# Constant matmuls on TensorE ahead of the early jobs' products, in a gated scan followed by a two-level mixture of experts

## The chip, the cores and the metric

One core of a Trainium2 chip. The time is device microseconds of one execution. The engines are called TensorE (PE in the rows, PEld its weight loads), VectorE (DVE), ScalarE (ACT), GpSimd (POOL) and SyncE (SP).

## The reference

Over a batch of 4 sequences of 3648 steps with 256 channels, a gated recurrence gives `y`; its 14592 rows are the tokens of a mixture of experts. Each token takes the best of 4 groups and in it the best of 4 experts, so one of 16 experts, and its row is run through that expert's two products.

```python
for t in range(S):                       # gated scan, f = lb + (1 - lb) * sigmoid(f_logit)
    h = f[:, t] * h + (1 - f[:, t]) * x[:, t]
    y[:, t] = h
# x = y as 14592 tokens
g_idx = argmax(x @ w_group); e_idx = argmax(xg @ w_expert[g])
h  = np.maximum(xg[mask_e] @ w1[g, e], 0.0)       # 256 -> 1024
ye = h @ w2[g, e]                                 # 1024 -> 256
out[tok_idx] = (g_w * e_w)[:, None] * ye
```

## The kernel before

**Two kinds of work run side by side.** The scan and the routing go over 29 units of 512 tokens: load of `zt` (z and x), tanh and affine on ScalarE, gate (L210, L230) and scan `h` (L221) on VectorE, transposes of `h` (L248) and routing products (L262, L273) on TensorE, the routing itself in small VectorE operations (L283 to L339) with a counting product on TensorE (L308 and L309, whose result VectorE reads into `both`, L331), and an indirect store that sorts the tokens' rows by expert into the list `xs`. The experts' work is cut into jobs. There are 16 early jobs (kind "A"), one for each expert, that take the first two to six tiles of 128 tokens of an expert as soon as enough units are routed (the table `EARLY`), and 16 later ones (kind "B") for the rest. Early jobs thus run while the scan goes on, up to about 270 us.

**A job.** Its rows come back from `xs` as `xr` (L760, on SyncE's queue), are transposed on TensorE (L816) and split into a float16 and a bfloat16 part, `xh` and `xl` (L821 ScalarE, L822 VectorE). Its weights come in four pieces `st`, split the same way into `wh` (L775 ScalarE) and `wl` (L776 VectorE). The first product (`m1_step`, L850 to L852, three matmuls for each exact one) fills a PSUM bank `ps_m` with 12 matmuls of 256 columns; ScalarE makes `hh` from it (L855) and VectorE `hl` (L856), and only then is the bank free. There are three such banks in turn (tag "m1"), and a job of 256 tokens needs four, so its fourth bank needs the `hl` of its first. The second product (`m2_step`, L869, 24 matmuls for 128 tokens) reads `hh` and `hl` into a bank of tag "m2" (two in turn). Transposes and routing products take a bank of tag "p" (three in turn).

**Order.** The second product of a job stands in the program behind the first product of the next job. Between the steps `bg_step` puts pieces of the scan and of the next job's preparation in. Up to the preparation of the first job the order on TensorE, VectorE and ScalarE is the program's; after that a scheduler orders these engines, by its own estimates, ahead of the run, and each engine then works its list strictly in order. `tri` and `upto` are two constant 128 by 128 masks in bfloat16, made once at the start.

Of the kernel before, what the change touches and what calls it, by code (L numbers as in the profile page):

```python
# [18 lines left out]
P = 128  # L19
NE = 16  # L20
UNIT = 512
# [19 lines left out]
def gated_scan_moe(ctx: ExitStack, tc, zx, lower, wroute, wexp, out, S):  # L41
    nc = tc.nc
# [5 lines left out]
    KF = F // P  # L48
# [21 lines left out]
    def bank(tag):  # L70
        return ps.tile([P, UNIT], F32, name=f"ps_{tag}", tag=tag, bufs=PS_BUFS[tag])
# [49 lines left out]
    tri = const.tile([P, P], BF16, name="tri")  # L121
    nc.gpsimd.tensor_scalar(out=tri, in0=dmat, scalar1=0.0, scalar2=None, op0=ALU.is_gt)
    upto = const.tile([P, P], BF16, name="upto")
# [548 lines left out]
    def make_job(kind, idx):  # L672
        j = Job()
        j.kind, j.idx = kind, idx
        j.len = EARLY[idx][1] * P if kind == "A" else CAPS[idx] if kind == "B" else P
        j.tiles = -(-j.len // P)
        j.chunks, j.pieces, j.cols, j.parts = [], [], [], []
        at = 0
        while at < j.len:
            rest = j.len - at  # L680
            w = 2 * P if rest > 3 * P else P if rest > 2 * P else rest
            n = UNIT // w
            j.cols.append([list(range(c, min(KF, c + n))) for c in range(0, KF, n)])
            j.pieces += [(b, min(2 * P, at + w - b)) for b in range(at, at + w, 2 * P)]
            parts, b = [], at
            while b < at + w:
                m = at + w - b
                g = 1 if m > 96 else 2 if m > 32 else 4
                parts.append((b, min(m, P // g), g))
                b += P // g  # L690
            j.chunks.append((at, w))
            j.parts.append(parts)
            at += w
        j.wh, j.wl, j.st = {}, {}, {}
        j.hh, j.hl = {}, {}
        j.xh, j.xl = {}, {}
        return j
# [134 lines left out]
    def w2_at(ws, c):  # L832
        return ws[2 + c // 4][:, (c % 4) * D:(c % 4 + 1) * D]

    def m1_step(j, ch, cs):
# [11 lines left out]
        for n, c in enumerate(cs):  # L847
            po = pm[:, n * w:(n + 1) * w]
            for k in range(KD):
# [6 lines left out]
        nc.vector.scalar_tensor_tensor(out=j.hl[ch][:, cs[0]:cs[-1] + 1, 0:w], in0=pv, scalar=0.0, in1=hi,  # L856
                                       op0=ALU.max, op1=ALU.subtract)

    def m2_step(j, ch, t):
        b, p, g = j.parts[ch][t]  # L860
        pm = bank("m2")
        c0 = b - j.chunks[ch][0]
        q, dw = P // g, D // g
        n = p if g == 1 else q
        ts = slice(c0, c0 + n)
        for c in range(KF):
            for s, (h, w) in enumerate(((j.hh, j.wh), (j.hh, j.wl), (j.hl, j.wh))):
                for i in range(g):
                    nc.tensor.matmul(pm[i * q:i * q + n, 0:dw], h[ch][:, c, ts], w2_at(w, c)[:, i * dw:(i + 1) * dw],  # L869
                                     start=(c == 0 and s == 0), stop=(c == KF - 1 and s == 2),  # L870
                                     tile_position=(0, i * q) if g > 1 else None)
        o = mo.tile([P, D], F32, name="o", bufs=O_BUFS)
        if j.kind == "B":
            lt, r = j.info, b // P
            if g > 1:
                r += j.tails.index((b, p, g))
        else:
            pi = max(i for i, (a, _) in enumerate(j.pieces) if a <= b)
            lt, r = j.meta[pi], (b - j.pieces[pi][0]) // P
        s = slice(0, p if g == 1 else P)  # L880
        nc.scalar.activation(o[s, 0:dw], pm[s, 0:dw], AF.Copy, scale=lt.bitcast(F32)[s, r, 1:2])  # L881
        nc.gpsimd.indirect_dma_start(  # L882
            out=out_v[out_n[0]].rearrange("n (g d) -> (n g) d", g=g),
            out_offset=bass.IndirectOffsetOnAxis(ap=lt[s, r, 0:1], axis=0),
            in_=o[s, 0:dw], in_offset=None, bounds_check=g * N - 1, oob_is_err=False)
        out_n[0] += 1
# [22 lines left out]
    def bg_pop():  # L909
        done[0] += 1  # L910
        bgq.popleft()()

    def bg_to(n):
        while done[0] < n:
            bg_pop()

    def fetch_to(n):
        while pptr[0] < min(n, len(pieces)):
            j, i = pieces[pptr[0]]
            if j.kind != "A":  # L920
                bg_to(marks["order"])
            job_weights(j, i)
            pptr[0] += 1
# [3 lines left out]
    def prep_thunks(j):  # L927
        th = []

        def sp(i):  # L930
            if i == 2:
                live[0] += 1
            fetch_to(piece_index[(id(j), i)] + STG_BUFS)
            job_split(j, i)
            if i == 3 and j.kind == "B" and j.idx == 1:
                leftovers()
            if i == 3 and j.kind == "B" and j.idx + 1 < NE:
                tail_blank(j.idx + 1)

        for i in range(4):  # L940
            f = lambda i=i: sp(i)
            f.held = i == 2
            th.append(f)
        for pi in range(len(j.pieces)):
            th.append(lambda pi=pi: job_xt(j, pi))
        return th

    def start_macro(mi):
        mac = macros[mi]
        bg_to(marks[EARLY[mac[0].idx][0]] if mac[0].kind == "A" else marks["order"])  # L950
        for j in mac:
            if j.kind != "A" or j.idx == NE - 1:
                job_rows(j)
# [30 lines left out]
    with tc.manual_schedule(engines={mybir.EngineType.PE, mybir.EngineType.DVE, mybir.EngineType.Activation}):  # L984
        for u, n in EARLY_FETCH:
            while u not in last_load:
                bg_pop()
            fetch_to(n)
        bg_to(first)
        start_macro(0)  # L990
        prep = prep_thunks(macros[0][0])
        bg_to(marks["begun"])
        for t in prep:
            t()
    pending = None
    for mi, mac in enumerate(macros):
        q = deque()
        if mi + 1 < len(macros):
            start_macro(mi + 1)
            for j in macros[mi + 1]:  # L1000
                q.extend(prep_thunks(j))
        left = work(mac)
        for j in mac:
            for ch in range(len(j.chunks)):
                for cs in j.cols[ch]:
                    m1_step(j, ch, cs)
                    left -= len(cs)
                    bg_step(q, left - 2, len(cs))
                if pending is not None:
                    pj, pc = pending  # L1010
                    for t in range(len(pj.parts[pc])):
                        m2_step(pj, pc, t)
                        left -= 1
                        bg_step(q, left - 2, 1)
                    if pc == len(pj.chunks) - 1:
                        live[0] -= 1
                pending = (j, ch)
        while q:
            q.popleft()()
    pj, pc = pending  # L1020
    in_order.enter_context(tc.manual_schedule(engines={mybir.EngineType.Pool}))
    for t in range(len(pj.parts[pc])):
        m2_step(pj, pc, t)
    left = nc.values_load(regs["left"][0:1, 0:1], min_val=0, max_val=NT)
    in_order.close()
    with tc.For_i(0, left, 1) as it:
        ent = mo.tile([1, 3], I32, name="ent")
        rem = mo.tile([P, 1], F32, name="rem")
        sync.dma_start(out=ent, in_=tab[bass.ds(it + len(EXTRA_AT), 1), :])
        sync.dma_start(out=rem, in_=tab.bitcast(F32)[bass.ds(it + len(EXTRA_AT), 1), 2:3].broadcast_to([P, 1]))  # L1030
        j = make_job("X", 0)
        regs["tabs"], regs["xrem"] = ent, rem
        job_rows(j)
        for i in range(4):
            job_weights(j, i)
        for i in range(4):
            job_split(j, i)
        job_xt(j, 0)
        for cs in j.cols[0]:
            m1_step(j, 0, cs)  # L1040
        m2_step(j, 0, 0)
# [44 lines left out]
```

## Time and profile before

| | |
|---|---|
| time, median of 3 runs | 774.7 us (774.45 to 777.17) |
| the profiled execution | 776.18 us, span 774.4 us |
| TensorE busy | 715.7 us, 92% of the span |
| VectorE busy | 538.7 us, 70% |
| ScalarE busy | 461.4 us, 60% |
| mean granted TensorE clock | 0.96 |

A group of rows below is one view of the trace of that execution; times in it count from the start of its span. A matmul's busy time is longer than the step from one start to the next, since matmuls overlap; the step is what counts for a sum.

### The profile page before, as it was taken

Reading aid. Unit: us, or ns where it says so; the run is one execution under the profiler, and the core shown is the slowest. Engines: PE = TensorE matmul, PEld = TensorE weight load, DVE = VectorE, ACT = ScalarE, POOL = GpSimd, SP = SyncE. Lnnn points to the kernel's source line nnn. Section 1 sums busy time; section 2 is a strip of 40 time slices with the busy share of each in tenths; the row PEclk is TensorE's granted clock in tenths of the full one; section 3 lists DMA queues with packets and bytes.
Section 4 is the critical chain, followed back from the end, with each engine's and each line's share of the span. In section 5 each row is a group of like instructions: output and inputs, shape, how many; then the busy total and the mean of one; then the engine's idle time right before and its main releaser. Section 6 shows DMA issues by size and latency. Waiting matters only on the chain.

```text
span 774.4 us, 20888 instructions
## 1 busy us (share of the span) xinstructions
PE 715.7 (92%) x8112; PEld 634.0 (82%) x8112; DVE 538.7 (70%) x1058; ACT 461.4 (60%) x824; POOL 289.4 (37%) x272
## 2 busy tenths in 40 slices
PE   2655679999999999999999999999999999999995
PEld 1434567888888888989988898999999999999995
DVE  6889899999999966865555544555564676656540
ACT  6667777987888846454455444454555465555541
POOL 3671264577556453541211222213222322232222
PEclk9955889999999999999999999999999999999998
DMA  7997879999998826378535344453563555555300
GB/s 276 355 347 262 313 245 344 328 314 354 336 311 301 271 96 185 122 238 215 123 116 126 129 99 129 114 129 118 140 173 96 166 151 173 165 164 173 86 30 24
DMA packets 93157, 151.75 MB, mean 196 GB/s; under 512 B 52417, under 2 KB 62559, under 8 KB 89728
## 3 DMA queue, kind: packets, MB, share of 16 engines
q1 hardware_dynamic: 78080, 99.90, 43.5%
q0 software_dynamic: 11424, 30.02, 11.0%
q10 hardware_dynamic: 3552, 20.48, 7.3%
q8 instruction: 64, 1.05, 0.6%
q14 instruction: 37, 0.30, 0.1%
HBM read 112.69 MB, written 38.19 MB: 195 GB/s over the span
## 4 chain that ended last, share of the span: by engine, by line
PE 56%; DVE 19%; DMA 11%; issue 7%; ACT 3%; POOL 2%; SPq 1%; POOLq 0%; DVEq 0%; ACTq 0%
PE ps_m L869 28%; PE ps_m L850 6%; DVE wl L776 6%; PE ps_m L851 6%; PE ps_m L852 6%; DMA zt<-in_zx_dram 5%; DVE h L221 4%; PE ps_p L850 3%; PE ps_p L851 3%; PE ps_p L852 3%; DVE hl L856 3%; DMA st<-in_wexp_dram 2%; DVE zt L210 2%; DMA xs<-blank 2%; POOL out_dram L882 2%
## 5 line engine op out<-in xcount | busy, mean ns | idle before, releaser
L869 PE MATMUL ps_m<-wh,hl 128*128 128x256 f16 (+2 forms) x1320 | 265.7, 251 | 4.7 <-DVE hl L856 4.6
L869 PE MATMUL ps_m<-wl,hh 128*128 128x256 bf16 (+2 forms) x1320 | 265.7, 251 | 0.1
L869 PE MATMUL ps_m<-wh,hh 128*128 128x256 f16 (+2 forms) x1320 | 265.4, 252 | 0.2 <-ACT hh L855 0.2
L869 PEld LDWEIGHTS <-hh 128*128 128x128 f16 (+2 forms) x2640 | 195.6, 99 | 23.6 <-issue 3.3
L850 PE MATMUL ps_m<-xh,wh 128*128 128x256 f16 (+11 forms) x782 | 197.4, 263 | 2.7 <-DVE hl L856 2.7
L851 PE MATMUL ps_m<-xl,wh 128*128 128x256 bf16 (+11 forms) x782 | 197.4, 262 | 1.0 <-DVE xl L822 1.0
L852 PE MATMUL ps_m<-xh,wl 128*128 128x256 f16 (+11 forms) x782 | 197.4, 262 | 0.0
L776 DVE TENSOR_TENSOR wl<-st,wh 128x1024 bf16<-128x1024 f32 x128 | 154.3, 1219 | 51.3 <-ACT wh L775 51.1
L343 POOL DMA_INDIRECT xs<-rows,posi x114 | 133.3, 1169 | 123.8 <-DVE rows L325 45.3
L882 POOL DMA_INDIRECT out_dram<-o,info x75 | 86.1, 1148 | 242.5 <-ACT o L881 214.3
L856 DVE SCALAR_TENSOR_TENSOR hl<-ps_m,hh 128x512 bf16<-128x512 f32 (+6 forms) x176 | 117.4, 670 | 70.3 <-ACT hh L855 69.9
L855 ACT ACTIVATE hh<-ps_m 128x512 f16<-128x512 f32 (+6 forms) x176 | 103.5, 588 | 72.5 <-PE ps_m L852 70.7
L775 ACT CAST wh<-st 128x1024 f16<-128x1024 f32 x128 | 132.1, 1046 | 14.1 <-PE ps_m L869 7.6
L869 PEld LDWEIGHTS <-hl 128*128 128x128 bf16 (+2 forms) x1320 | 104.6, 99 | 15.3 <-DVE hl L856 5.0
L850 PEld LDWEIGHTS <-wh 128*128 128x128 f16 x1088 | 107.2, 99 | 11.0 <-issue 1.6
L851 PEld LDWEIGHTS <-wh 128*128 128x128 f16 x1088 | 107.4, 99 | 10.5 <-issue 2.4
L852 PEld LDWEIGHTS <-wl 128*128 128x128 bf16 x1088 | 107.2, 98 | 9.4 <-issue 1.2
L882 POOL DMA_INDIRECT out_dram<-o,meta x55 | 65.5, 1192 | 111.6 <-ACT o L881 101.0
L881 ACT ACTIVATE o<-ps_m,info 128x256 f32<-128x256 f32 (+4 forms) x75 | 33.1, 441 | 83.8 <-PE ps_m L869 74.3
L850 PE MATMUL ps_p<-xh,wh 128*128 128x256 f16 (+13 forms) x306 | 73.3, 252 | 0.0
L851 PE MATMUL ps_p<-xl,wh 128*128 128x256 bf16 (+13 forms) x306 | 73.3, 252 | 0.0
L852 PE MATMUL ps_p<-xh,wl 128*128 128x256 f16 (+13 forms) x306 | 73.3, 252 | 0.0
(145 smaller groups left out, 741.2 us busy)
## 6 DMA issues: line engine op xcount, KB each, us to landing
st<-in_wexp_dram SPq DMA_DIRECT2D x128, 512.0 KB, 7.2
zt<-in_zx_dram ACTq DMA_DIRECT2D x19, 1024.0 KB, 7.5
zt<-in_zx_dram SPq DMA_DIRECT2D x7, 1024.0 KB, 9.8
xs<-blank SPq DMA_DIRECT2D x26, 258.0 KB, 4.4
xr<-xs SPq DMA_DIRECT2D x19, 258.0 KB, 6.0
xr<-xs SPq DMA_DIRECT2D x17, 129.0 KB, 4.1
xs<-rows,posi POOLq DMA_INDIRECT x114, 7.1
zt<-xs SPq DMA_DIRECT2D x8, 152.0 KB, 3.2
```

The costliest lines, as they stand in the source:

```text
L221: nc.vector.tensor_tensor_scan(out=h[:, k, c0 - a:c1 - a], data0=ff[:, k, c0 - a:c1 - a], data1=uu[:, k, c0 - a:c1 - a], initial=init, op0 ...
L343: sc = nc.gpsimd.indirect_dma_start(out=xs_v[G["t0"] + t][:, :], out_offset=bass.IndirectOffsetOnAxis(ap=R["posi"][:, t:t + 1], axis=0), i ...
L775: nc.scalar.copy(j.wh[i], j.st[i])
L776: nc.vector.tensor_tensor(out=j.wl[i], in0=j.st[i], in1=j.wh[i], op=ALU.subtract)
L850: nc.tensor.matmul(po, w1_at(j.wh, k, c), xh[:, k], start=(k == 0), stop=False)
L851: nc.tensor.matmul(po, w1_at(j.wh, k, c), xl[:, k], start=False, stop=False)
L852: nc.tensor.matmul(po, w1_at(j.wl, k, c), xh[:, k], start=False, stop=(k == KD - 1))
L855: nc.scalar.activation(hi, pv, AF.Relu)
L856: nc.vector.scalar_tensor_tensor(out=j.hl[ch][:, cs[0]:cs[-1] + 1, 0:w], in0=pv, scalar=0.0, in1=hi, op0=ALU.max, op1=ALU.subtract)
L869: nc.tensor.matmul(pm[i * q:i * q + n, 0:dw], h[ch][:, c, ts], w2_at(w, c)[:, i * dw:(i + 1) * dw], start=(c == 0 and s == 0), stop=(c == ...
L881: nc.scalar.activation(o[s, 0:dw], pm[s, 0:dw], AF.Copy, scale=lt.bitcast(F32)[s, r, 1:2])
L882: nc.gpsimd.indirect_dma_start(out=out_v[out_n[0]].rearrange("n (g d) -> (n g) d", g=g), out_offset=bass.IndirectOffsetOnAxis(ap=lt[s, r, ...
```

## The change

A function `keep_warm` puts `n` matmuls of the two constants (128 columns, bfloat16) into the last quarter of a bank, whose result nobody reads. It is called with 46 ahead of the first job's preparation, with 48 in the middle of the second product of the first job (first tile, into a bank "p" of its own), and with 24 at the head of the second product of the second and of the third job (first tile, into the bank that the product then fills). 142 matmuls and as many weight loads are added. The lists of the engines change with them.

```diff
@@ -856,14 +856,23 @@
         nc.vector.scalar_tensor_tensor(out=j.hl[ch][:, cs[0]:cs[-1] + 1, 0:w], in0=pv, scalar=0.0, in1=hi,
                                        op0=ALU.max, op1=ALU.subtract)
 
+    def keep_warm(pm, n):
+
+        for _ in range(n):
+            nc.tensor.matmul(pm[:, UNIT - P:UNIT], tri, upto, start=True, stop=True)
+
     def m2_step(j, ch, t):
         b, p, g = j.parts[ch][t]
         pm = bank("m2")
+        if j.kind == "A" and j.idx in (1, 2) and t == 0:
+            keep_warm(pm, 24)
         c0 = b - j.chunks[ch][0]
         q, dw = P // g, D // g
         n = p if g == 1 else q
         ts = slice(c0, c0 + n)
         for c in range(KF):
+            if j.kind == "A" and j.idx == 0 and t == 0 and c == KF // 2:
+                keep_warm(bank("p"), 48)
             for s, (h, w) in enumerate(((j.hh, j.wh), (j.hh, j.wl), (j.hl, j.wh))):
                 for i in range(g):
                     nc.tensor.matmul(pm[i * q:i * q + n, 0:dw], h[ch][:, c, ts], w2_at(w, c)[:, i * dw:(i + 1) * dw],
@@ -990,6 +999,7 @@
         start_macro(0)
         prep = prep_thunks(macros[0][0])
         bg_to(marks["begun"])
+        keep_warm(bank("m2"), 46)
         for t in prep:
             t()
     pending = None
```

**TensorE, ahead of the first job.** L248 and L262 are transposes and routing of the scan, L816 the transposes of the first job's rows. Before:

```order
L262 MATMUL ps_p<-h,wr 32x128 x8
L273 MATMUL ps_p<-ident,rs 128x128
L248 MATMUL ps_p<-ident,h 128x128 x8
L816 MATMUL ps_p<-ident,xr 128x128 x4
L248 MATMUL ps_p<-ident,h 128x128 x4
L262 MATMUL ps_p<-h,wr 32x128 x8
L850 LDWEIGHTS wh_813
```

Of the change (L862 is `keep_warm`):

```order
L273 MATMUL ps_p<-ident,rs 128x128
L248 MATMUL ps_p<-ident,h 128x128 x8
L862 LDWEIGHTS tri
L862 MATMUL ps_m_813<-upto,tri 128x128
...
L862 MATMUL ps_m_813<-upto,tri 128x128
L816 MATMUL ps_p<-ident,xr 128x128 x4
L248 MATMUL ps_p<-ident,h 128x128 x4
L262 MATMUL ps_p<-h,wr 32x128 x8
```

The 46 stand between the last transposes of the scan and those of the first job's rows.

**TensorE, at the third job's first product.** The program's 48 of the first job's second product come here. The numbers in the names differ between the two kernels: `ps_m_1492` and `ps_m_1550` of before are `ps_m_1588` and `ps_m_1646` of the change, the third job's first and second bank. Before:

```order
L262 MATMUL ps_p<-h,wr 32x128 x8
L850 LDWEIGHTS wh_1291
L850 MATMUL ps_m_1492<-xh,wh_1291 128x256
L850 LDWEIGHTS wh_1291
L850 MATMUL ps_m_1550<-xh,wh_1291 128x256
L248 MATMUL ps_p<-ident,h 128x128 x4
L851 LDWEIGHTS wh_1291
L851 MATMUL ps_m_1492<-xl,wh_1291 128x256
```

Of the change:

```order
L850 LDWEIGHTS wh_1338
L850 MATMUL ps_m_1588<-xh,wh_1338 128x256
L850 LDWEIGHTS wh_1338
L850 MATMUL ps_m_1646<-xh,wh_1338 128x256
L862 LDWEIGHTS tri
L862 MATMUL ps_p<-upto,tri 128x128
...
L862 MATMUL ps_p<-upto,tri 128x128
L248 MATMUL ps_p<-ident,h 128x128 x4
L851 LDWEIGHTS wh_1338
L851 MATMUL ps_m_1588<-xl,wh_1338 128x256
```

The 48 stand between the first matmul into the second bank and the L248 transposes, ahead of the other eleven matmuls of each bank.

**VectorE, from the fourth job's weight splits on.** `wl` is a weight split (L776), the rows from `both` to `rows` are the twelve small operations of the routing, `hl` from `ps_m_1492`, `ps_m_1550` and `ps_m_1595` is that of the third job's first three banks (`ps_m_1588`, `ps_m_1646` and `ps_m_1691` of the change). Before:

```order
L776 TENSOR_TENSOR wl_1510<-st,wh_1509 128x1024
L776 TENSOR_TENSOR wl_1516<-st,wh_1515 128x1024
L856 SCALAR_TENSOR_TENSOR hl<-ps_m_1492,hh 128x512
L776 TENSOR_TENSOR wl_1568<-st,wh_1567 128x1024
L856 SCALAR_TENSOR_TENSOR hl<-ps_m_1550,hh 128x512
L776 TENSOR_TENSOR wl_1574<-st,wh_1573 128x1024
L331 TENSOR_TENSOR both<-ps_p,both 128x32
...
L325 RECIPROCAL rows<-s_1627 128x4 x2
L856 SCALAR_TENSOR_TENSOR hl<-ps_m_1595,hh 128x512
L210 SCALAR_TENSOR_TENSOR zt<-zt 128x1024
L822 TENSOR_TENSOR xl<-ps_p,xh 128x512
```

Of the change:

```order
L776 TENSOR_TENSOR wl_1606<-st,wh_1605 128x1024
L776 TENSOR_TENSOR wl_1612<-st,wh_1611 128x1024
L776 TENSOR_TENSOR wl_1664<-st,wh_1663 128x1024
L776 TENSOR_TENSOR wl_1670<-st,wh_1669 128x1024
L331 TENSOR_TENSOR both<-ps_p,both 128x32
...
L325 RECIPROCAL rows<-s_1723 128x4 x2
L856 SCALAR_TENSOR_TENSOR hl<-ps_m_1588,hh 128x512
L856 SCALAR_TENSOR_TENSOR hl<-ps_m_1646,hh 128x512
L856 SCALAR_TENSOR_TENSOR hl<-ps_m_1691,hh 128x512
L210 SCALAR_TENSOR_TENSOR zt<-zt 128x1024
```

The two `hl` that stood between and behind the last weight splits now stand behind these and behind the routing operations, next to the third.

## Rows read from the trace of the kernel before

**Rows 1.** The page's first part, busy time of each engine with its share of the span, and the granted TensorE clock in 40 slices, in tenths of full speed.
```profile
PE 715.7 (92%) x8112; PEld 634.0 (82%) x8112; DVE 538.7 (70%) x1058; ACT 461.4 (60%) x824; POOL 289.4 (37%) x272
...
PEclk9955889999999999999999999999999999999998
```

**Rows 2.** Busy time by stretch (us from the span's start): the stretch, its length, then for TensorE, its weight load, VectorE, ScalarE and GpSimd the busy us and instructions, then granted clock, share of the DMA engines and GB/s.
```profile
68.00:77.00 9.00, 8.39 (x48) 6.07 (x49) 9.00 (x11) 6.07 (x12) 0.00 (x0) 0.50 0.81 247
...
90.00:101.00 11.00, 6.20 (x36) 4.55 (x33) 10.19 (x19) 5.01 (x12) 8.48 (x8) 0.53 0.73 230
101.00:115.00 14.00, 10.78 (x99) 8.12 (x98) 13.79 (x29) 12.26 (x23) 9.05 (x7) 0.88 0.75 234
115.00:126.00 11.00, 9.00 (x67) 7.32 (x66) 11.00 (x14) 9.14 (x17) 3.26 (x4) 0.84 1.00 344
126.00:274.00 148.00, 146.31 (x1526) 129.87 (x1525) 144.95 (x269) 121.09 (x226) 90.38 (x71) 1.00 0.91 316
274.00:720.00 446.00, 445.54 (x5261) 405.06 (x5260) 263.80 (x528) 230.20 (x393) 127.45 (x114) 1.00 0.51 144
```

**Rows 3.** Who waited for whom: engine, tile and line, what it waited for, then us in total, times, longest. The first five rows are of 65 to 126 us (TensorE's for row loads, for `hl` and for `xl`, and VectorE's for TensorE), the last two are all of TensorE's from 126 to 274.
```profile
PE ps_p L816 <- DMA xr<-xs: 8.8, 3, 5.7
PE ps_m L869 <- DVE hl L856: 4.6, 1, 4.6
...
PE ps_m L850 <- DVE hl L856: 1.1, 1, 1.1
PE ps_m L851 <- DVE xl L822: 1.0, 1, 1.0
...
DVE both L331 <- PE ps_p L309: 2.2, 2, 1.6
...
PE ps_m L850 <- DVE hl L856: 1.2, 2, 0.9
PE ps_p L262 <- DVE both L331: 0.4, 1, 0.4
```

**Rows 4.** TensorE's instructions in order of time: start, us, line, operation, output and inputs, count, and in brackets the idle time ahead with what ended it.
```profile
60.53 1.92 PE L248 MATMUL ps_p<-ident,h 128*128 128x128 f32 x8
68.17 1.32 PE L816 MATMUL ps_p<-ident,xr 128*128 128x128 f32 x4 [5.72 <-DMA xr<-xs]
...
72.91 0.37 PE L851 MATMUL ps_m<-xl,wh 128*128 128x256 bf16 x1
...
74.57 0.42 PE L850 MATMUL ps_m<-xh,wh 128*128 128x256 f16 x1
74.78 0.42 PE L851 MATMUL ps_m<-xl,wh 128*128 128x256 bf16 x1
```

**Rows 5.** VectorE's instructions around the first `both` of the early jobs, columns as above.
```profile
79.17 0.42 DVE L301 TENSOR_TENSOR_SCAN scn<-rmask,oh 128x128 bf16<-128x128 bf16 x1
81.19 0.19 DVE L331 TENSOR_TENSOR both<-ps_p,runoff 128x32 f32<-128x32 f32 x1 [1.59 <-PE ps_p L309]
```

**Rows 6.** TensorE's instructions around the third early job's four banks (the first at 114.55, the second at 115.98, the fourth at 123.70) and the first matmul of the fourth job at 132.29.
```profile
115.98 0.27 PE L850 MATMUL ps_m<-xh,wh 128*128 128x256 f16 x1 [1.15 <-DVE hl L856]
116.09 0.60 PE L248 MATMUL ps_p<-ident,h 128*128 128x128 f32 x4
117.71 0.27 PE L851 MATMUL ps_m<-xl,wh 128*128 128x256 bf16 x1 [1.03 <-DVE xl L822]
...
123.70 0.27 PE L850 MATMUL ps_m<-xh,wh 128*128 128x256 f16 x1
...
132.29 0.27 PE L850 MATMUL ps_m<-xh,wh 128*128 128x256 f16 x1
```

**Rows 7.** VectorE's instructions over the same time; `hl` at 122.86 is that of the third job's first bank (`ps_m_1492`), at 124.59 of its second, at 128.14 of its third.
```profile
120.61 2.34 DVE L776 TENSOR_TENSOR wl<-st,wh 128x1024 bf16<-128x1024 f32 x2
122.86 0.69 DVE L856 SCALAR_TENSOR_TENSOR hl<-ps_m,hh 128x512 bf16<-128x512 f32 x1
123.46 1.22 DVE L776 TENSOR_TENSOR wl<-st,wh 128x1024 bf16<-128x1024 f32 x1
124.59 0.69 DVE L856 SCALAR_TENSOR_TENSOR hl<-ps_m,hh 128x512 bf16<-128x512 f32 x1
125.19 1.22 DVE L776 TENSOR_TENSOR wl<-st,wh 128x1024 bf16<-128x1024 f32 x1
126.33 0.19 DVE L331 TENSOR_TENSOR both<-ps_p,both 128x32 f32<-128x32 f32 x1
...
128.14 0.66 DVE L856 SCALAR_TENSOR_TENSOR hl<-ps_m,hh 128x512 bf16<-128x512 f32 x1
```

**Rows 8.** TensorE's instructions, first and last of 48 matmuls with 128 columns that follow one another without a pause.
```profile
191.73 0.22 PE L850 MATMUL ps_m<-xh,wh 128*128 128x128 f16 x1
...
194.35 0.22 PE L852 MATMUL ps_m<-xh,wl 128*128 128x128 f16 x1
```

**Rows 9.** Busy time by stretches of 5 us, columns as in group 2: two around pauses of TensorE and one ahead.
```profile
45.00:50.00 5.00, 4.30 (x32) 2.93 (x32) 4.79 (x12) 3.31 (x9) 3.86 (x4) 0.50 1.04 402
...
90.00:95.00 5.00, 0.76 (x8) 0.31 (x4) 4.83 (x9) 2.77 (x7) 3.72 (x4) 0.56 0.84 260
95.00:100.00 5.00, 4.44 (x23) 3.50 (x24) 4.36 (x8) 1.24 (x4) 3.78 (x5) 0.50 0.59 176
100.00:105.00 5.00, 4.34 (x45) 3.24 (x43) 4.86 (x15) 4.85 (x10) 1.86 (x2) 0.92 0.48 183
```


## The prediction

> **What bounds the kernel now.** Three views, in this order. The page says how full the engines are: TensorE is busy for 92% of the span and VectorE for 70% [rows 1]. That is an average, so the second view cuts the span where it changes character [rows 2]. Before 126 us TensorE is never full, and the granted clock stands at 0.50 to 0.88 of full speed. VectorE is full: 9.00 of 9.00 us from 68 to 77, 13.79 of 14 and 11.00 of 11 from 101 to 126. From 126 to 274 both are full (146.31 and 144.95 of 148). After 274 TensorE alone is full, 445.54 of 446 us. So whatever TensorE is late by at 274 arrives at the end undiminished, and before 126 a faster TensorE wins only where VectorE waited for it. The third view names those waits [rows 3]. From 65 to 126 TensorE loses 8.8 us to row loads (`xr<-xs`), 4.6 and 1.1 us to VectorE's `hl` and 1.0 us to its `xl`; VectorE loses 2.2 us to TensorE. From 126 to 274 TensorE waits 1.2 us for `hl` and 0.4 us for `both`, and that is all.
>
> The profiled execution took 776.18 us with a span of 774.4, 1.8 us lying around it; its time is 1.5 us above the median of 774.7. I work out a difference on that execution and add it to the median.
>
> **The change part by part.** It adds 142 matmuls, 128 columns wide in bf16, and removes nothing. A matmul of that width at full clock starts 0.0557 us after the one before: 48 of them between 191.73 and 194.35 [rows 8]. At half clock 256 columns take 0.213 us (74.57 to 74.78), so 128 take 0.107 [rows 4].
>
> *The first 46.* TensorE ends its transposes at 62.4 and starts the next at 68.17, after 5.72 us of waiting for a load; 46 at 0.107 us take 4.9 us and end at 67.3 [rows 4]. Cover is complete: cost 0. Were the load 2 us earlier, 1.1 us would show. What can they win? The matmuls behind them wait for VectorE's `xl` until 72.91 anyway [rows 4]. Only then could a higher clock help, and what it helps is `both`: VectorE has its scan done at 79.6, waits 1.59 us for L309 and goes on at 81.19 [rows 5]. If the clock is still full at 72.9, nearly all of that goes: -1.3 us. If not, the order puts three more matmuls of 0.11 us ahead of L308: +0.3 us. I take -0.5, near the middle but closer to nothing. The reason: between 45 and 50 us TensorE was busy for 4.30 of 5 us with transposes and routing work and the clock stayed at 0.50 [rows 9], and it is just such work that stands between the 46 and 72.9. The Trainium skill says likewise, in "TensorE: Matmul & The Clock Gate", Part 4: PE-mode transpose, that transposes don't count as a busy engine does; the trace agrees with its 0.50 at 4.30 busy. By that rule alone the term would be +0.3 and the time 0.8 us longer than mine.
>
> *The 48.* They were written into the first job's second product, where TensorE stood 4.6 us for `hl` [rows 3], but the order puts them later: behind the first matmul into `ps_m_1646`, which is `ps_m_1550` of before, at 115.98 [rows 6]. What waits is behind them on TensorE: the L248 transposes and the remaining matmuls of the third job. There the cover is the 1.03 us wait for `xl`; the 48 take 48 x 0.0557 = 2.7 us at full clock. TensorE also worked at half clock for a while: 0.84 granted over the 11 us from 115 to 126 is 1.8 us short of full [rows 2], and most of that may be spared. So by itself this part costs little. But the order of VectorE changes with it. Before, it made `hl` from `ps_m_1492` at 122.86 between the weight splits, ending 123.5, and TensorE's fourth bank of that job (`ps_m_1651`), which needs that bank back, starts at 123.70: it was just in time [rows 6, 7]. Now two more splits and twelve small routing operations come first. VectorE has no pause here, so times follow by adding: splits done at 122.86, two more of 1.13 (123.46 to 124.59) to 125.12, the small ones 1.81 (126.33 to 128.14) to 126.93, and `hl` 0.67 to 127.6 [rows 7]. TensorE gets there about 123.9 (116.09 + 2.7, then the work of before from 117.71 to 123.70 without its half-clock loss of 1.7, and two L248 groups of 0.44 ahead of it) and stands for 3.7 us. Its fourth bank starts at 127.65: **+3.95 us**. Bounds: 0 if VectorE is 4 us earlier by then, which its 2.2 us of waits don't allow, and +4.3 with the +0.3 from above.
>
> *The 24 of the second job.* Three are ahead of that stall and hidden in it. The other 21 come behind: 1.17 us. The wait of 0.4 for `both` is gone and the L248 group of 0.44 us now lies in the stall: together **+0.3 us**.
>
> *The 24 of the third job* stand ahead of 48 matmuls in a stretch where TensorE has no pause: 24 x 0.0557 = **+1.3 us**, with no cover.
>
> *What comes back.* TensorE being the late one, its 1.2 us of waits for `hl` until 274 go: **-1.2 us**; at worst none of it comes back.
>
> *The clock behind the new stall.* The row of 90 to 95 us, with a pause of 4.6 us in it, shows 0.56, the next 0.50 and the third 0.92 [rows 9]: from the end of the pause at 95.56 to about 100.8 TensorE ran at half rate, which cost 2.6 us. So 0 to 2.6; I take **+0.8**, since the new pause is shorter and the matmuls right behind it are dense.
>
> Sum: -0.5 + 3.95 + 0.3 + 1.3 - 1.2 + 0.8 = +4.65 us; 774.7 + 4.7 = **779.4 us**. With the lower bounds but the stall kept: -1.3 + 3.95 + 0.3 + 1.3 - 1.2 + 0 = +3.0; with the upper (+0.3, +2.6): +7.2.
>
> **The rivals.**
> *The additions only fill.* If VectorE reaches the moved `hl` as TensorE does (it makes up its 2.2 us, or the wait of TensorE for its bank is shorter than I count), the 96 late matmuls cost 5.35 us, less 1.0, 0.4 and 1.2 us of waits that they fill, 1.7 us of half clock and 0.5: +0.5, **775.2 us**. For it: VectorE's total of work is unchanged. Against: its rows from 115 to 128 leave no gap. It decides if the `hl` in question ends before about 125.
>
> *Faster.* TensorE's clock is what matters from 68 to 126. At full clock throughout, 4.2 us come back of 8.39 busy from 68 to 77, 2.5 from 90 to 101, 1.7 of 14 at 0.88 and 1.8 of 11 at 0.84 [rows 2]: 10 us, less the 3.7 us of late matmuls without a wait to fill: -6.3, **768.4 us**. The Trainium skill, in the same page under "Why this matters for your kernels", advises to keep TensorE busy and without long pauses so that it keeps its full rate; by that rule this is the case. Against: VectorE is full in each of those stretches and its order is fixed, so TensorE could not use what it gained beyond VectorE's 2.2 us of waits. It decides if VectorE can be ahead of now by over 4 us at 126.
>
> *Stalls that breed.* TensorE 4.3 us late hands `hh` of the fourth job over late, VectorE, in order, stands about 2.9 us (adding on from 127.6 it would reach that `hl` near 135.9, and TensorE's bank, begun at 132.29 + 4.3, gives `hh` near 138.8), and routing and splits behind it are late; if this comes back to TensorE once more with its half-rate price, 2.8 us are added: **782.2 us**. Against: the banks later on have some us to spare once TensorE is the late one.
>
> **How the numbers follow.** Forecast case 0.45 (776.9 to 781.5), only filling 0.30, breeding stalls 0.16, faster 0.09. A measurement here tells about 0.5% from no change, 3.9 us: 770.8 to 778.6 is "same". Of the forecast case two thirds lie above 778.6. Slower: 0.30 + 0.16 = 0.46; same: 0.15 + 0.29 = 0.44; faster: 0.09 and 0.01 of the filling case, 0.10. The range of 773.0 to 783.0 leaves out the faster case and the far end of the breeding one, some 0.14.
>
> **What would show it.** Right: 46 short matmuls between 62.4 and 67.4 with the load still ending the wait at about 68; the 48 between 115 and 119; TensorE idle 2 to 4 us before an L850, ended by `hl` L856, around 124 to 128; a lower granted clock in the 5 us behind that; TensorE 4 to 6 us behind before at 145 us, and no waits for `hl` until 274. Wrong: no such idle time; or the wait at L331 around 81 gone and VectorE over 2 us ahead at 115; or TensorE waiting for `hl` again at several places after 150.

## The result, and the profile after

The change is slower: 781.87 us, median of 7 runs (780.44 to 785.03), against 776.34 us for the kernel before in 7 runs. The medians differ by 5.5 us; the ratio of the runs is 1.0086, 95% interval 1.0069 to 1.0104, some 6.7 us. The forecast was 4.65 us on a base of 774.7, which 26 later runs put at 775.88. The profiled execution took 782.97 us with a span of 781.2, 6.8 us more than the one before. A ratio leaves out runs over 1.5% above the fastest of their kernel, which takes away a third of the runs of the kernel before where it takes 817 us (10 of 29 and 6 of 20), so that ratios from there can differ from those of the medians by up to 0.8%.

The page's first part of the change, busy time by engine and the granted clock in 40 slices (before: [rows 1]):

```profile
PE 723.7 (93%) x8254; PEld 642.4 (82%) x8254; DVE 539.1 (69%) x1058; ACT 462.6 (59%) x824; POOL 289.1 (37%) x272
...
PEclk9999779999999999999999999999999999999998
```

Busy time by stretch of the change, columns as in [rows 2]; the last two stretches end 6 and 7 us later than there, as the work does:

```profile
68.00:77.00 9.00, 6.15 (x60) 4.90 (x61) 9.00 (x10) 7.26 (x13) 0.00 (x0) 1.00 0.84 250
90.00:101.00 11.00, 7.06 (x41) 5.32 (x42) 10.19 (x20) 5.80 (x13) 8.26 (x8) 0.57 0.69 197
101.00:115.00 14.00, 10.07 (x78) 7.49 (x76) 13.79 (x30) 11.44 (x21) 9.32 (x8) 0.76 0.74 252
115.00:126.00 11.00, 9.57 (x121) 8.48 (x121) 11.00 (x21) 10.56 (x20) 3.55 (x3) 1.00 1.02 388
126.00:280.00 154.00, 151.07 (x1576) 133.86 (x1576) 145.28 (x261) 120.16 (x221) 88.59 (x71) 0.99 0.86 295
280.00:727.00 447.00, 446.55 (x5271) 405.99 (x5270) 263.52 (x528) 231.33 (x396) 127.40 (x114) 1.00 0.51 146
```

The clock of 68 to 77 us went from 0.50 to 1.00, and VectorE, which sets the pace there, was full before and is full now. Behind 280 us nothing differs but the start.

The mean clocks of the two executions (0.960 before, 0.983 now) can't be compared: the clock record of this trace begins at 65.3 us, that of the trace before at 29.1, and a stretch without a record counts as full. The fourth slice above shows a 9, but the eight transposes ahead of the 46 take as long as at the 0.50 of before (1.92 us, [rows 4]):

```profile
61.49 1.91 PE L248 MATMUL ps_p<-ident,h 128*128 128x128 f32 x8
63.19 3.74 PE L862 MATMUL ps_m<-upto,tri 128*128 128x128 bf16 x46
```

TensorE's instructions of the change from the third early job's third bank on, and where the two groups of 24 end up, columns as in [rows 6]:

```profile
122.78 0.64 PE L816 MATMUL ps_p<-ident,xr 128*128 128x128 f32 x4
124.80 0.66 PE L248 MATMUL ps_p<-ident,h 128*128 128x128 f32 x4 [1.38 <-DVE both L331]
125.29 0.33 PE L862 MATMUL ps_m<-upto,tri 128*128 128x128 bf16 x3
...
127.08 0.37 PE L850 MATMUL ps_m<-xh,wh 128*128 128x256 f16 x1 [1.13 <-DVE hl L856]
127.25 0.42 PE L851 MATMUL ps_m<-xl,wh 128*128 128x256 bf16 x1
127.47 0.42 PE L852 MATMUL ps_m<-xh,wl 128*128 128x256 f16 x1
...
130.49 1.35 PE L862 MATMUL ps_m<-upto,tri 128*128 128x128 bf16 x21
...
137.35 0.27 PE L850 MATMUL ps_m<-xh,wh 128*128 128x256 f16 x1
...
144.73 1.50 PE L862 MATMUL ps_m<-upto,tri 128*128 128x128 bf16 x24
...
194.44 0.27 PE L850 MATMUL ps_m<-xh,wh 128*128 128x256 f16 x1 [1.41 <-DVE hl L856]
```

The fourth bank, at 123.70 before [rows 6], starts at 127.08, and TensorE stands twice in front of it: for `both`, then for `hl`. The matmuls behind it follow at 0.21 us, half rate, where they stood at 0.11. The fourth job starts at 137.35 against 132.29.

VectorE's instructions of the change over the same time (before: [rows 7]):

```profile
120.03 4.60 DVE L776 TENSOR_TENSOR wl<-st,wh 128x1024 bf16<-128x1024 f32 x4
124.56 0.18 DVE L331 TENSOR_TENSOR both<-ps_p,both 128x32 f32<-128x32 f32 x1
...
126.37 1.85 DVE L856 SCALAR_TENSOR_TENSOR hl<-ps_m,hh 128x512 bf16<-128x512 f32 x3
...
139.49 0.69 DVE L856 SCALAR_TENSOR_TENSOR hl<-ps_m,hh 128x512 bf16<-128x512 f32 x1 [3.69 <-ACT hh L855]
```

Four splits in a row, then the routing, then three `hl`: VectorE loses nothing by it until 130 us. At 139.49 it has waited 3.69 us for the `hh` of a bank that TensorE began late. The waits of 126 to 280 us, TensorE's and VectorE's:

```profile
PE ps_m L850 <- DVE hl L856: 2.7, 3, 1.4
...
DVE hl L856 <- ACT hh L855: 5.5, 4, 3.7
```

TensorE's 1.2 us for `hl` [rows 3] have become 2.7, of which 1.13 belong to the stall itself. Behind it, the longest wait of before (0.9 us, at 273.7 us) is gone, and one of 1.41 at 194.44 has come.

**Where the time went.** Start against start of the same work, after less before, in the two profiled executions: VectorE 0.95 later at 60 us, ahead of the first added matmul, and 0.70 at 66 us; 0.58 earlier from 82 us on, once its wait in front of `both` is down from 1.59 [rows 5] to 0.32; TensorE 0.45 earlier at the third job's third bank, 3.38 later at the fourth, 5.06 at the fourth job, 6.40 behind the third job's 24, 7.6 over most of 200 to 240 us, 6.86 from 281 us to the end.

### The profile page after: what moved, and what is told of

Same layout as the page of the kernel before. It is cut to its first block, busy times and chain, and to the rows that moved or that the text cites. A ratio compares the mean times of both kernels' runs of the same rounds, so it can differ in the third digit from the quotient of the medians.

```text
span 781.2 us, 21168 instructions
## 1 busy us (share of the span) xinstructions
PE 723.7 (93%) x8254; PEld 642.4 (82%) x8254; DVE 539.1 (69%) x1058; ACT 462.6 (59%) x824; POOL 289.1 (37%) x272
## 4 chain that ended last, share of the span: by engine, by line
PE 62%; DVE 15%; DMA 10%; issue 8%; ACT 2%; POOL 2%; SPq 1%; POOLq 0%; DVEq 0%; ACTq 0%
PE ps_m L878 30%; PE ps_m L850 7%; PE ps_m L852 7%; PE ps_m L851 7%; DMA zt<-in_zx_dram 4%; DVE wl L776 3%; DMA st<-in_wexp_dram 3%; PE ps_p L850 3%; PE ps_p L851 3%; PE ps_p L852 3%; DVE h L221 3%; DVE hl L856 2%; POOL out_dram L891 2%; DVE zt L210 1%; PE ps_p L248 1%
## 5 line engine op out<-in xcount | busy, mean ns | idle before, releaser
L776 DVE TENSOR_TENSOR wl<-st,wh 128x1024 bf16<-128x1024 f32 x128 | 154.3, 1218 | 52.6 <-ACT wh L775 52.4
L891 POOL DMA_INDIRECT out_dram<-o,meta x55 | 63.8, 1160 | 127.3 <-ACT o L890 110.4
```

Of the source, the lines that this page charges most:

```text
L776: nc.vector.tensor_tensor(out=j.wl[i], in0=j.st[i], in1=j.wh[i], op=ALU.subtract)
L891: nc.gpsimd.indirect_dma_start(out=out_v[out_n[0]].rearrange("n (g d) -> (n g) d", g=g), out_offset=bass.IndirectOffsetOnAxis(ap=lt[s, r, ...
```

## The experiments

Two questions: is it the matmuls or the order that they brought with them, and which part of the order. So that the second can be asked without the first, most kernels hold TensorE, VectorE and ScalarE to a written list by edges that fix the order and add no wait:

```
+    def pin(order):
+        for eng, seq in order.items():
+            mine = [i for i in traced if i.engine == eng]
+            for a, b in zip(seq, seq[1:]):
+                tc.add_manual_dep(mine[b], mine[a].name, <order only>)
```

"Old lists" are those of before (but for one or two exchanged neighbours), "new lists" those of the change; the size of each of the four groups is set apart. Held lists keep the second job's 24 together.

Six runs (old_lists_all, new_lists_one, hl_put_back, first46 and the second run of the first and the last) fell on chips on which the kernel before takes 776 us, twelve on chips on which it takes 811 to 817 us. On the slower chips TensorE stands all over the trace without waiting for anything that the profile shows ("issue"): in the change run there, 9.1 us in the second products behind 280 us alone. The trace of the kernel before is that of a 776 us run and has no such wait behind 126 us. So each ratio is taken against the kernel before on the same chip, and each place in a trace is compared after VectorE's shift just ahead of it is taken off.

**Order or matmuls.** old_lists_all: old lists, all 142.

```
+    pin({PE: OLD, DVE: OLD, Activation: OLD})
```

> All 142 matmuls as in the change, at the same places of TensorE's list, but TensorE, VectorE and ScalarE are held, by order-only edges, to the lists that these engines have when each of the four groups is a single matmul; those are the lists of the kernel before but for one or two exchanged neighbours. So this prices the matmuls without the new order. My theory (the new order makes the loss): the sum of the case of only filling, +0.5 us, to +1.5 if the spared half clock of 1.7 us does not come; ratio 1.000 to 1.002; TensorE's fourth bank of the third job less than 1.5 us later than before. Rival (the matmuls themselves are the loss, the order only follows): +5 to +7 us, ratio 1.006 to 1.009.

778.77 us, ratio 1.0040 (1.0025 to 1.0056). TensorE's trace:

```profile
114.66 0.27 PE L916 MATMUL ps_m<-xh,wh 128*128 128x256 f16 x1 [0.98 <-DVE hl L922]
114.77 2.84 PE L947 MATMUL ps_p<-upto,tri 128*128 128x128 bf16 x48
...
122.28 0.27 PE L916 MATMUL ps_m<-xh,wh 128*128 128x256 f16 x1
...
131.95 0.27 PE L916 MATMUL ps_m<-xh,wh 128*128 128x256 f16 x1
```

No stall: the fourth bank at 122.28 is 1.42 us ahead of before, as the second bank was by 1.32 in front of the 48. The second job's 24 take that to 0.33 ahead at the fourth job, the third job's 24 to 1.01 behind at 146 us, and it stays at 1.0 to the end. (This execution, 777.25 us, is 1.5 us under the median.)

new_lists_one: new lists, four matmuls in all.

```
+    pin({PE: NEW, DVE: NEW, Activation: NEW})
-        keep_warm(bank("m2"), 46)
+        keep_warm(bank("m2"), 1)
...
-                keep_warm(bank("p"), 48)
+                keep_warm(bank("p"), 1)
```

and the 24 likewise.

> The counterpart: the three engines are held to the lists of the change, but each group is one matmul (4 in all instead of 142). So this prices the new order without the matmuls. My theory: TensorE still stands 3 to 5 us before the third job's fourth bank, its clock falls behind that stall, and the kernel is 3.5 to 6 us slower than before, ratio 1.0045 to 1.008. Rival (the matmuls are the loss): 0 to 1 us slower, ratio under 1.0015.

782.49 us, ratio 1.0085 (1.0063 to 1.0108): all of the change's loss, with 4 of its 142 matmuls. TensorE's two waits are there, the first longer since no 48 stand in front:

```profile
124.91 0.66 PE L311 MATMUL ps_p<-ident,h 128*128 128x128 f32 x4 [2.79 <-DVE both L394]
...
127.19 0.37 PE L913 MATMUL ps_m<-xh,wh 128*128 128x256 f16 x1 [1.24 <-DVE hl L919]
```

So the order makes the loss, and the matmuls in their places add little to it, though the clock was at half for longer behind this stall than in the change (0.51 against 0.66 from 126 to 131 us), which may make up for some of their cost. In the old lists they cost more than nothing; a repeat, old_lists_all_b:

> The kernel of old_lists_all again. Theory (46 and 48 free, 24 and 24 cost 2.4 us): ratio 1.0015 to 1.0045. Rival (nothing but filling: 0.5 us): 1.001 or less.

778.53 us, ratio 1.0029 (1.0014 to 1.0043), some 2 to 3 us as expected. Its profiled execution, 782.80 us and the slowest of the 12, shows the other end: the clock was 0.50 from 115.8 to 122.6 us, the 48 took 5.33 us instead of 2.84, and the fourth bank started 3.50 us later than before where VectorE was 0.93 later. So the 48 are covered at full clock and not at half.

**Which part of the order.** hl_put_back: the change, with two `hl` back in their old places on VectorE (and, by the holding, all 24 of the second job in front of the bank, which its expectation does not say). VectorE's held list:

```
 wl split 1, wl split 2
+hl of the first bank
 wl split 3
+hl of the second bank
 wl split 4
 both L331, the routing
-hl of the first bank, hl of the second bank
 hl of the third bank
```

> The change with all 142 matmuls and its lists, but with the hl of the third job's first and second bank put back on VectorE to where the kernel before has them, behind the second and behind the third of the four weight splits; nothing else moves. The prediction made this one instruction the stall of 3.95 us. If that is right, TensorE's fourth bank starts near 124 us, and the time is 3 to 4 us under the change, about 778 us, ratio to before 1.002 to 1.004. Rival, from the trace of the change: TensorE first waits for both L331 at 124.80 us, in front of an L248 group that the new list puts ahead of that bank, and with two hl of 0.6 us ahead of it both comes 1.2 us later; then L248 starts near 126.0, the fourth bank near 127.15 against 127.08, and the time stays within 0.7 us of the change, ratio 1.008 to 1.0095.

779.82 us, ratio 1.0052 (1.0034 to 1.0070). At the bank:

```profile
123.20 1.50 PE L944 MATMUL ps_m<-upto,tri 128*128 128x128 bf16 x24
125.77 0.41 PE L325 MATMUL ps_p<-h,wr 128*32 128x128 f32 x2 [1.07 <-DVE both L394]
126.11 0.28 PE L913 MATMUL ps_m<-xh,wh 128*128 128x256 f16 x1
```

`hl` is done at 122.7 and the bank still starts at 126.11: 2.41 us later than before where VectorE is 0.79 ahead, 3.2 in all, against 3.96 in the change. `both`, which now comes behind the two `hl`, holds it. That is the rival's cause, though the wait stands in front of two matmuls of L262 and not of the L248 group, and the rival had the bank near 127.15 and the time within 0.7 us of the change. The time falls by 2.1 us against the change (medians of separate timings), more than the 0.8 won at the bank. Two more things differ: the 21 of the 24 that stood behind the bank (1.17 us) now lie in the stall, and the clock did not fall behind this pause, 1.00 from 126 to 131 where the change has 0.66 and new_lists_one 0.51:

```profile
126.00:131.00 5.00, 5.00 (x55) 4.12 (x54) 4.96 (x16) 2.82 (x5) 2.86 (x3) 1.00 1.02 375
```

tensor_list_back: the change with the old list on TensorE alone.

```
+    pin({PE: OLD, DVE: NEW, Activation: NEW})
```

> The change with all 142 matmuls and with its lists on VectorE and ScalarE, but TensorE held to its list of before, in which the third job's fourth bank stands ahead of the L248 group that waits for both. hl_put_back moved the other half. Theory (two locks on one door: the moved hl and the moved L248 group each hold that bank until 126 to 127 us, so that opening one alone gains little at the bank): the fourth bank still starts 3 to 4 us later than before, waiting for hl; the time is within 2 us of the change, ratio 1.006 to 1.009. Rival (TensorE's list was the cause): the bank starts at most 1 us later than before, ratio 1.002 to 1.004.

836.06 us, ratio 1.0209 (1.016 to 1.0257), and the change itself, change_again, on another of the slower chips:

> The change as it is, beside the three below. Where the kernel before takes about 776 us: ratio 1.007 to 1.0105, as in its first timing, with the fourth bank of the third job 3.4 to 4.2 us later than before, start shift aside. Where the kernel before takes about 817 us: 1.02 to 1.03 if the new order is what costs there too, since fill_the_stall, which has that order, read 1.0275; 1.010 or less if the loss there belongs to the held lists.

825.14 us, ratio 1.0198 (1.0153 to 1.0242): the loss is there too, twice as large. The bank of tensor_list_back:

```profile
131.45 0.40 PE L918 MATMUL ps_m<-xh,wh 128*128 128x256 f16 x1 [3.93 <-DVE rows L393]
```

It is 7.75 us later than before where VectorE is 3.80 later: the same 3.95, now in one wait, for the `hl` right behind `rows`. So there are two locks on one door, and its ratio, too, agrees with that of the change within the intervals. both_open takes off both: `hl_put_back`, and on TensorE the bank ahead of L248.

```
 L816 of the next rows
+12 matmuls of the fourth bank
 L248 group, the 24, one of L262
-12 matmuls of the fourth bank
 the rest of L262
```

> The change's lists with all 142 matmuls, with both holds on the third job's fourth bank taken off: hl of the first and second bank put back on VectorE as in hl_put_back, and on TensorE the twelve matmuls of the fourth bank in front of the L248 group, as in the kernel before. Theory: the bank starts within 0.6 us of before's 123.70, start shift aside, TensorE then waits under 1.5 us for both, and the kernel is 1 to 1.5 us under hl_put_back, ratio 1.0032 to 1.0045, what is left being the matmuls' own 2.4 us and the rest of the new lists. Rival (what costs lies in the lists behind 130 us): no gain on hl_put_back, ratio 1.005 or more.

823.66 us, ratio 1.0159 (1.0104 to 1.0215), median against median 1.0076; once more beside change_again, both_open_b:

> The kernel of both_open again. Theory: 3.5 to 5 us under the change, and the fourth bank less than 0.6 us later than before, start shift aside; what is left is the matmuls' own 2.4 us and the rest of the new lists. Rival (the loss lies in the lists behind 130 us): less than 2.5 us under the change though the bank starts in time.

821.05 us, ratio 1.0133 (1.0094 to 1.0171), 4.1 us under the change. Its bank starts when the transposes are through, with no wait:

```profile
126.70 0.64 PE L879 MATMUL ps_p<-ident,xr 128*128 128x128 f32 x4
127.32 0.27 PE L913 MATMUL ps_m<-xh,wh 128*128 128x256 f16 x1
```

3.61 us later than before, VectorE 3.61 later: not a tenth of the stall is left. So the two holds make the stall. Its opening gave 4.1 us of time, within the 3.5 to 5 expected, but the two intervals overlap; the bank's start is what shows it. What it would give on a chip of the faster kind was not run. Against the zero point on that chip, 0.9994, some 10 us remain: the 24s and the new lists behind 130 us, which were not taken apart.

fill_the_stall: new lists, all 142, the second job's 24 wholly in the stall.

```
+    pin({PE: NEW, DVE: NEW, Activation: NEW})   # 3 + 21 become 24 + 0
```

> The change with its own lists on all three engines, but the second job's 24, of which 3 stand in front of the third job's fourth bank and 21 behind it, all stand in front of it, in the stall. Theory (the stall is filled at no cost and the clock does not fall): the fourth bank still starts 3.4 to 4 us later than before, the 21 behind it are gone (1.2 us), and the half rate behind the stall (1.7 us in the change) goes too: 1.2 to 2.9 us under the change, ratio to before 1.0045 to 1.0075, granted clock 1.00 from 127 to 131 us. Rival (the clock falls all the same, by the waits of 1.4 and 1.1 us that are still not wholly filled): only the 1.2 us, ratio 1.007 or more.

835.51 us, ratio 1.0275 (1.022 to 1.033); one of its six runs took 4134 us, and the median of the other five is 833.05. Beside the change, fill_the_stall_b:

> The kernel of fill_the_stall again, beside the change. Theory (the 21 matmuls that move into the stall are free there, and the clock is kept): 1.2 to 2.9 us under the change. Rival (the clock falls all the same, or holding the lists costs): not under the change by more than 1.2 us.

827.35 us, ratio 1.0218 (1.0180 to 1.0257), not under the change. The clock did hold (1.00 from 131 to 137, 0.72 in change_again), but TensorE then waited on "issue" five times by 0.33 to 1.02 us between 139 and 144 us, where change_again has two such waits of 0.32 and 0.17 us. The theory failed, and the runs can't say why.

**The zero point and the parts.** old_lists_one: the held lists of old_lists_all, the four groups of 1 matmul each as in new_lists_one.

> The lists of before again, with a single matmul in each of the four places: the zero point for the two runs below, and the price of holding the lists with edges. Theory: nothing here costs more than 4 x 0.06 us; ratio 0.999 to 1.001. Rival (the edges or the one or two exchanged neighbours cost what old_lists_all lost): ratio 1.003 to 1.005.

Ratio 1.0031 (0.9988 to 1.0073). Repeated as old_lists_one_b:

> The kernel of old_lists_one again, for the same reason: the zero point of the lists of before held with edges and four single matmuls. Theory: ratio 0.999 to 1.001. Rival (holding the lists costs something itself): 1.003 to 1.005.

1.0078 (1.0038 to 1.0117), and a third time, old_lists_one_c:

> The kernel of old_lists_one again, the zero point. Theory: ratio 0.999 to 1.002. Rival (holding the lists with edges costs by itself, as the 1.003 and 1.008 of its two runs hint): 1.003 or more, and then old_lists_all's 1.004 is the edges and not the matmuls.

0.9994 (0.9971 to 1.0017). The second and the third disagree by more than their intervals, so on these chips a ratio tells nothing below 0.8%; the narrowest says that holding the lists is free. old_lists_46 and old_lists_46_b have 46 again in the first place (`keep_warm(bank("m2"), 46)`):

> The lists of before with the first 46, and one matmul in each of the other three places. first46 came out 0.42% slower, where I had expected a gain, and its trace shows no gain of VectorE (hl 1.9 us later than before at 95 us, 1.3 of it there before the 46) and a pause of 1.97 us with nothing waited for at 696 us. Theory (the 46 leave the clock to chance between 72 and 77 us: it was 0.50 there in first46 and 0.97 in old_lists_all, worth -1.3 to +0.6 us, and the late pause belongs to first46's one execution): ratio 0.9985 to 1.001. Rival (the 46 themselves are slow for a reason not seen yet): ratio 1.003 to 1.005, as first46.

> The kernel of old_lists_46 again: that run was made where the kernel before took 816.85 us, with waits on issue of 2 to 5 us all over the trace, and told nothing below 0.4%. The same expectation: ratio 0.9985 to 1.001 if the 46 only leave the clock between 72 and 77 us to chance; 1.003 to 1.005 if they are slow by themselves, as first46 came out.

1.0030 (0.9988 to 1.0073) and 1.0083 (1.0043 to 1.0122), each within 0.0005 of the old_lists_one or old_lists_one_b run beside it: by themselves the 46 cost nothing that shows within intervals of 0.4%. old_lists_96, the 48 and both 24s without the 46:

> The lists of before with the 48 and both groups of 24, and one matmul in place of the first 46. By the trace of old_lists_all the 48 cost nothing (TensorE 1.32 us ahead of before at the bank in front of them, 1.45 at the next), the second job's 24 cost 1.1 and the third job's 1.34, and none of it comes back until the end. Theory: +2.4 us, ratio 1.002 to 1.004, and TensorE 2.2 to 2.6 us later than before, start shift aside, from 150 us to the end. Rival (the prediction's: 1.2 us come back as TensorE's waits for hl go): +1.2 us, ratio 1.0005 to 1.002.

1.0069 (1.0026 to 1.0113), 0.0038 above old_lists_one beside it where 0.003 was expected; too wide to decide.

first46: the change with the 46 alone, no list held.

```
-            if j.kind == "A" and j.idx == 0 and t == 0 and c == KF // 2:
-                keep_warm(bank("p"), 48)
-        if j.kind == "A" and j.idx in (1, 2) and t == 0:
-            keep_warm(pm, 24)
```

> Only the 46 in front of the first early job's transposes are left; the 48 and both 24s are out. The lists of VectorE and ScalarE are then those of the kernel before, instruction by instruction, and TensorE's differs by six places. My theory (the first 46 are covered and win VectorE's wait for L309 around 81 us at most): 0.5 to 1.3 us faster, a ratio of 0.998 to 0.999, VectorE 0.6 to 1.3 us ahead at its hl around 115, and no new wait at the third job. Rival (a full clock from 63 to 77 us carries on and speeds up all that follows): 3 us or more faster, ratio under 0.996. Rival (the 46 are part of what made the change slower): slower by 1 us or more.

778.62 us, ratio 1.0042 (1.0022 to 1.0063): a miss, slower where faster was expected. Again, first46_b:

> The kernel of first46 again. Theory (the 46 cost nothing, and first46's 1.0042 is partly chance): ratio 0.998 to 1.002. Rival (the 46, or the six exchanged places of TensorE's list, cost about 3 us): 1.003 or more.

777.58 us, ratio 1.0028 (1.0008 to 1.0048): a miss again. The traces of the two profiled executions show two things. First, 72 to 77 us was at half rate (first46, and the change under it):

```profile
72.00:77.00 5.00, 4.15 (x32) 2.54 (x21) 5.00 (x7) 2.48 (x5) 0.00 (x0) 0.50 0.99 321
```

```profile
72.00:77.00 5.00, 3.72 (x33) 3.29 (x34) 5.00 (x6) 3.33 (x8) 0.00 (x0) 1.00 0.88 291
```

and VectorE waited 1.86 and 1.77 us for L309, not less than 1.59. Second, both stand at the same matmul, some 690 us in, with nothing waited for; first46, then first46_b:

```profile
696.11 0.20 PE L874 MATMUL ps_m<-wl,hh 128*32 128x64 bf16 x2 [1.97 <-issue]
```

```profile
696.82 0.21 PE L874 MATMUL ps_m<-wl,hh 128*32 128x64 bf16 x2 [2.52 <-issue]
```

That is 3.5 and 2.5 us of lateness gained there (the clock fell behind the first of the two), most of what these two executions lost. But they took 781.75 and 780.86 us, 3.1 and 3.3 us above the medians of their runs, so whether the median run, 2.7 and 1.5 us above the kernel before, has the pause is not shown, and the cause of that loss stays open. Why this program stands there and the others on those chips do not was not tried.

## Why the prediction came out as it did

*Right* were the place and the size of the stall: 3.95 us were forecast and 3.83 measured (TensorE from 0.45 ahead to 3.38 behind). It was right, too, that VectorE would not stand idle for it, that the 48 and the first 46 are covered (in the profiled execution of the change; at half clock the 48 are not, old_lists_all_b), that the third job's 24 cost 1.3 (1.34, from 5.06 to 6.40), and that a faster TensorE ahead of 115 us wins only VectorE's waits. The filling case fell with the `hl` ending at 127, the faster case with VectorE 1.3 us ahead and not 4.

*The step that failed: "What comes back".* It took 1.2 us off because TensorE, being the late one, would no longer wait for `hl`. Between the third job's 24 and the end TensorE lost 0.46 us more instead: 0.9 us of the old waits did go, and 1.41 us at 194.44 and smaller ones came. old_lists_all shows the flaw without the stall: TensorE is 1.01 late at 146 us, VectorE's next `hl` 1.07 late, and the lateness is 1.0 at the end. VectorE works its list in order and waits for `hh` of the late bank, so it becomes late by the same amount and the slack between the two is what it was. In the change it waited 5.5 us for `hh` and, as the traces read, handed 1.4 us back at 194.44; no run tests that step by itself. This is the breeding rival without its second half rate (the clock stayed full from 130.2 us to the last 6 us); the text had it at 782.2 us and 0.16, and that the time came so near is partly chance, since 0.70 us of it is a later start. On its mechanism it deserved about the chance of the forecast case, since the same paragraph had already worked out VectorE's wait (2.9 us forecast, 3.69 found) and then kept the 1.2 us all the same. The upper total kept it too: with "at worst none of it comes back" it would have been +8.45 and not +7.2.

*The clock behind the stall* was mis-sized, 0.8 us: twelve matmuls of 256 columns took 2.65 us where the kernel before has 1.31 of them, and the fourteen pieces of L262 some 0.25 more, 1.6 us in all. That the pause was shorter than the one of the rows was no ground for a third of the price: new_lists_one stayed at 0.51 for the 5 us behind, hl_put_back at 1.00.

*The cause of the stall* was half told. `hl` was named as the one that is late, and L248 counted as 0.44 us of work ahead of it. But the new list also puts two matmuls of L262 ahead of the fourth bank, and one or the other waits for the bank that `both` frees (L248 1.38 us in the change, L262 1.07 in hl_put_back). That was a second hold. Neither `hl` put back (0.8 us won at the bank) nor TensorE's list put back (nothing) opens it; taking off both does.

*The first 46* were put at -0.5, and the two ends at -1.3 and +0.3 were nearer to what happens. In nine of the fourteen profiled executions with the 46 VectorE gained 1.24 to 1.28 us between 72 and 95 us, in five it gained nothing or lost up to 0.7. But of the five executions with one matmul in their place two gained 1.27 us as well (old_lists_one_b, old_lists_one_c) and the others 0.22 to 0.63. With VectorE's shift taken off, the clock rose at 72.1 and 72.9 us in those two, at 74.7 to 76.4 in the other three and at 76.9 in the kernel before: the earlier it rose, the more was gained, and the 46 are not needed for it. So the gain can't be put down to them alone. The reason given, that the clock falls again behind the transposes, held in first46 (0.50) and not in the change (1.00). The Trainium skill, in "TensorE: Matmul & The Clock Gate", Part 4: PE-mode transpose, says that transposes do not count as a busy engine does; by that the clock would fall each time, and the change's 1.00 over 68 to 77 us, transposes first, does not agree.

Term by term, forecast and found: 46 and the waits up to the third bank -0.5 and -1.15; stall +3.95 and +3.83; second job's 24 with the clock +1.1 and +1.68; third job's 24 +1.3 and +1.34; what comes back -1.2 and +0.46. That is +4.65 and +6.16, and 0.70 of later start, which is chance. No version run here was faster than the kernel before by more than its interval.

## What to carry to other kernels

Work that is added for no result still goes through the scheduler: four matmuls in the new order cost what 142 did. Read the lists of every engine before the price of the instructions. Where an engine is late at one place, ask for each lock on that place, and take nothing off for waits "that will vanish" while the other engine works in order behind it, for it can be late too. A higher clock is worth the waits of the engine that sets the pace, no more: here TensorE's clock from 68 to 77 us rose from 0.50 to 1.00, and VectorE, busy for all 9.00 us, won 1.28 us. And see where the record of the clock begins before two means of it are compared.

## What the runs showed of the hardware

A pause of TensorE with nothing to wait for can sit at one matmul of a program and come again on another chip (1.97 and 2.52 us), where groups of four short matmuls of a job's tail follow each other at 0.03 us; 46 matmuls put in 630 us earlier were in front of it both times, and no other trace from those chips has it. The clock behind it fell once (0.50 from 697 to 699 us, behind 1.97) and once did not (1.00, behind 2.52), so the length of a pause alone does not tell. And chips differ: the kernel before took 776 us on two and 811 to 817 on three others, each used at one time only, so that chip and time can't be told apart; the change lost 0.86% in its first timing, where the kernel before took 776 us, and 1.98% where it took 811.
